# x in 64x64 quadrants of TensorE and a lag of four units, in a kernel of linear attention and a gated feed-forward layer

## The chip, the cores and the metric

One core of a Trainium2 chip. The metric is device time in microseconds (us), the median of several executions. Before: 284.53 us (four runs, 284.4 to 284.81).

Engines: PE is TensorE (PEld its weight loads), DVE is VectorE, ACT is ScalarE, POOL is GpSimd, SP issues transfers.

## The reference

```python
# q, k, v: (8 batches, 8 heads, 576 tokens, 64); w_in: 512 x 2048; w_out: 2048 x 512
q_s = softmax(q, over the 64 features);  k_s = softmax(k, over the 576 tokens)
kv  = einsum('bhsd,bhse->bhde', k_s, v)            # one 64x64 matrix a head
x   = einsum('bhsd,bhde->bhse', q_s, kv)           # -> 4608 tokens x 512
h   = x @ w_in
out = (h * sigmoid(beta * h)) @ w_out
```

The work is cut into nine chunks of 512 tokens: 512 tokens of each of the eight batches, and one chunk of the eight 64-token tails. Names used below: `kv` is the kv product of a batch; `x` the product of q and kv of a chunk, which gives the input of the feed-forward layer transposed, in four tiles kt of 128 features; `h j` (j = 0 to 15) are four matmuls that make 128 of the 2048 hidden features; `b j` are four matmuls that add hidden features j to four output accumulators (`acc`). Between h and b, ACT makes `th` (tanh of h) and DVE makes `g` from th and h.

## The kernel before

The kernel uses eight banks of PSUM. Four hold acc; of the others two serve h (tag "h") and two serve kv and x (tag "att").

x was made from weights of two heads side by side on the diagonal of a 128x128 tile whose other two quarters are zero (`kvp`), one full-array matmul for each kt:

```python
def xpe(c, j, tag):
    t = x_ps[c, j] = ps.tile([P, MAIN], F32, tag=bank(tag), ...)
    if c < B:
        nc.tensor.matmul(t[:], kvp[:, c, j, :], qsT[c][:, :, j, :])     # 128x128, 512 columns
        return
    for b in range(B):                                                  # the tails, 64 columns each
        i, e = divmod(b, 2)
        nc.tensor.matmul(t[:, ds(b * TAIL, TAIL)], kvp[:, b, j, :], qsT[B][:, i, j, ds(e * TAIL, TAIL)])
```

kv ran in two column tiles (128 rows by 64 columns), 40 matmuls of 65 columns:

```python
for i in range(R + 1):
    for e in range(2):
        hd = 2 * j + e
        nc.tensor.matmul(t[e * D : (e + 1) * D, jl, 0:D1], ek[...], va[...],
                         start=(i == 0), stop=(i == R), tile_position=(0, e * D))
```

A chunk made its 16 h units with b two units behind, and in between, through `side`, the softmaxes, kv and x of the next chunk:

```python
# h0 b14' h1 b15' h2 h3 b0 b1 h4 b2 h5 b3 ... h15 b13      (' = of the chunk before)
if u == 9 + (n == 1) and kb < B:
    kv_mm(kb, 0, n=HP); kv_norm(kb, 0, n=HP)
if 11 <= u < 15:                                  # one x after each of b9, b10, b11, b12
    j = u - 11
    x_mm(qc, j, nc.scalar if j % 2 == 0 else nc.vector)
```

The softmax here doesn't subtract the row's maximum and nothing guards it: scores larger than these inputs give would overflow.

Of the kernel before, what the change touches and what calls it, by code (L numbers as in the profile page):

```python
# [17 lines left out]
def kernel(  # L18
# [10 lines left out]
    nc = tc.nc  # L29
# [15 lines left out]
    FIX, LASTMAIN, COLT, XT4 = True, True, True, False  # L45
# [20 lines left out]
    kvp = const.tile([P, B, HP, P], BF16, name="kvp")  # L66
# [22 lines left out]
    def load_q(b, parts=1, only=None):  # L89
        if b not in q_st:  # L90
            q_st[b] = stage.tile([P, H, R * D], F32, tag="q_st", bufs=2, name=f"q_st{b}")
        t = q_st[b]
        src = q[b, :, 0:MAIN, :].rearrange("h (p i) d -> p h (i d)", i=R)
        n = H // parts
        for s in range(parts) if only is None else (only,):
            nc.sync.dma_start(t[:, s * n : (s + 1) * n, :], src[:, s * n : (s + 1) * n, :])  # L96
# [125 lines left out]
    def q_exp(b, s, n=2):  # L222
        if s == 0:
            eq[b] = work.tile([P, R, H, D], BF16, tag="eq", bufs=2, name=f"eq{b}")
        m = H // n
        nc.scalar.activation(  # L226
# [30 lines left out]
    HB, AB = ["b3", "b0"], ["b1", "b2"]  # L257
# [53 lines left out]
    def kv_mm(b, jj, n=2, tag="att"):  # L311
        t = ps.tile([P, n, D1 if b < NW or COLT else 2 * D1], F32, tag=bank(tag), bufs=1, name=f"kv{b}_{jj}")
        att_of[b, jj] = t
        for jl in range(n):
            j = n * jj + jl
            if b < NW:
                for i in range(RW):
                    for e in range(2):
                        r = slice(e * D, (e + 1) * D)
                        nc.tensor.matmul(  # L320
                            t[r, jl, 0:D1],
                            ek[b][r, j, ds(i * D, D)],
                            va[b][r, j, i, :],
                            start=(i == 0),
                            stop=(i == RW - 1),
                            tile_position=(e * D, e * D),
                        )
                continue
            if COLT:
                for i in range(R + 1):  # L330
                    for e in range(2):
                        hd = 2 * j + e
                        nc.tensor.matmul(  # L333
                            t[e * D : (e + 1) * D, jl, 0:D1],
                            ek[b][:, i, hd, :] if i < R else ekt[(b // 2) % 2][:, ds(hd * D, D)],
                            va[b][:, i, hd, :] if i < R else vt[(b // 2) % 2][:, b % 2, hd, :],
                            start=(i == 0),
                            stop=(i == R),
                            tile_position=(0, e * D),
                        )  # L340
                continue
            for i in range(R):
                nc.tensor.matmul(
                    t[:, jl, :],
                    ek[b][:, i, 2 * j : 2 * j + 2, :].rearrange("p h d -> p (h d)"),
                    va[b][:, i, 2 * j : 2 * j + 2, :].rearrange("p h d -> p (h d)"),
                    start=(i == 0),
                    stop=False,
                )
            nc.tensor.matmul(  # L350
                t[:, jl, :],
                ekt[(b // 2) % 2][:, ds(j * P, P)],
                vt[(b // 2) % 2][:, b % 2, 2 * j : 2 * j + 2, :].rearrange("p h d -> p (h d)"),
                start=False,
                stop=True,
            )

    def kv_norm(b, jj, n=2):
        t = att_of.pop((b, jj))
        rk = work.tile([P, n, 1], F32, tag="rk", bufs=2, name=f"rk{b}_{jj}")  # L360
        nc.vector.reciprocal(rk[:], t[:, :, D : D + 1])
        for e in range(2):
            r = slice(e * D, (e + 1) * D)
            dst = kvp[r, b, n * jj : n * jj + n, e * D : (e + 1) * D]
            src = t[r, :, 0:D] if b < NW or COLT else t[r, :, e * D1 : e * D1 + D]
            nc.vector.tensor_tensor(dst, src, rk[r].to_broadcast((D, n, D)), ALU.mult)
# [3 lines left out]
    def xpe(c, j, tag):  # L370
        t = x_ps[c, j] = ps.tile([P, MAIN], F32, tag=bank(tag), bufs=1, name=f"x{c}_{j}")
        if c < B:
            nc.tensor.matmul(t[:], kvp[:, c, j, :], qsT[c][:, :, j, :])  # L373
            return
        for b in range(B):
            i, e = divmod(b, 2)
            nc.tensor.matmul(  # L377
                t[:, ds(b * TAIL, TAIL)],
                kvp[:, b, j, :],
                qsT[B][:, i, j, ds(e * TAIL, TAIL)],  # L380
            )
# [6 lines left out]
    def x_mm(c, j, eng, tag="att"):  # L388
        xpe(c, j, tag)
        xev(c, j, eng)  # L390

    xp_of = {}

    def x_tiles(c):
        xp_of[c] = [ps.tile([P, HP, MAIN // 2], BF16, tag=bank("att"), bufs=1, name=f"xp{c}_{e}") for e in range(2)]
        for j in range(HP):
            for th in range(2):
                for e in range(2):
                    r = slice(e * D, (e + 1) * D)
                    nc.tensor.matmul(  # L400
                        xp_of[c][e][th * D : (th + 1) * D, j, :],
# [544 lines left out]
```

## Time and profile before

| | |
|---|---|
| time | 284.53 us |
| span of the profile | 282.9 us |
| PE busy | 97% |
| period of a middle chunk | 29.35 us |
| its 128 matmuls of h and b | 27.61 us |
| its kv block | 0.86 us |
| its four x | 0.86 us |

From the page of the kernel before: the busy times (engine, us, share of the span, instructions) and the chain of work that ended last.

```profile
PE 275.2 (97%) x1653; PEld 130.1 (46%) x1681; DVE 176.5 (62%) x274; ACT 164.9 (58%) x243; POOL 39.6 (14%) x60
...
PE 93%; DMA 3%; SPq 1%; POOL 1%; issue 1%; ACT 0%
PE h L425 44%; PE acc L473 42%; DMA v_st<-in_v_dram 3%; PE x L373 2%; PE kv L333 2%; PE acc L465 1%; PE kv L292 1%; SPq L122 1%; POOL va L161 0%; POOL w_in_b L161 0%; PE tp L273 0%; PE x L377 0%; SPq L119 0%; SPq L593 0%; SPq L96 0%
```

The chain is PE almost from end to end. "PE busy" alone would not say that PE is at its limit, since the matmuls' ends are modelled. The start times do. This is the PE timeline of the kernel before, around the kv block and the x of one middle chunk: start, us, engine, line, operation, count.

```profile
90.92 1.03 PE L473 MATMUL acc<-w_out_b,g 128*128 128x512 bf16 x4
91.88 0.32 PE L333 MATMUL kv<-va,ek 128*64 128x65 bf16 x8
...
92.50 0.20 PE L333 MATMUL kv<-vt,ekt 128*64 128x65 bf16 x2
92.64 1.04 PE L425 MATMUL h<-xT,w_in_b 128*128 128x512 bf16 x3
...
96.10 0.38 PE L373 MATMUL x<-qsT,kvp 128*128 128x512 bf16 x1
96.32 1.03 PE L425 MATMUL h<-xT,w_in_b 128*128 128x512 bf16 x4
97.18 1.03 PE L473 MATMUL acc<-w_out_b,g 128*128 128x512 bf16 x4
98.05 0.38 PE L373 MATMUL x<-qsT,kvp 128*128 128x512 bf16 x1
```

Read the differences of the first column. Four matmuls start in 97.18 - 96.32 = 0.86 us, 0.2157 us each: no gap. Below, a full matmul's "stream" is these 0.2157 us from its start. (The Trainium skill, TensorE: Matmul & The Clock Gate, section "Wait — 56ns, not 53.3ns?", gives N / 2.4 GHz plus about 2.5 ns for warm back-to-back matmuls, 215.7 ns at 512 columns. This trace agrees to the nanosecond.) An x takes 96.32 - 96.10 = 0.22, like any other full matmul, though half its weights are zeros. The kv block is entered 91.88 - (90.92 + 0.863) = 0.10 us later than a matmul of the same mode would have been, and left 0.13 us after its last start. That is what changing the tiling mode costs. A "x3" where four must be is a record missing from the trace, not a matmul left out.

The table by stretches (us, then each engine's busy time and instructions, PE clock, DMA share, GB/s) shows the slack of the others in a middle chunk:

```profile
core 0: us, PE busy (x) PEld busy (x) DVE busy (x) ACT busy (x) POOL busy (x), PEclk, DMA share, GB/s
...
93.68:123.03 29.35, 29.19 (x170) 13.55 (x172) 19.14 (x30) 17.43 (x25) 2.65 (x3) 1.00 0.63 171
```

### The profile page before, as it was taken

The numbers are of one execution on the slowest core, as the hardware profiler recorded it, in microseconds if no ns is written. First come the engines' busy times: TensorE is split into PE (matmuls) and PEld (weight loads), VectorE is DVE, ScalarE is ACT, GpSimd is POOL, SyncE is SP. The second block draws the span as 40 slices with busy tenths as digits, with TensorE's granted clock in tenths as the row PEclk, the third lists the DMA queues.
The fourth block names the chain that finished last, engine by engine and source line by source line (L and its number), as shares of the span: only waits on it lengthen the run. The fifth ranks groups of instructions, "written<-read, shape, count | busy, mean of one in ns | idle before, by whom it ended". The sixth has DMA issues, their size and how long they took to land.

```text
span 282.9 us, 4278 instructions
## 1 busy us (share of the span) xinstructions
PE 275.2 (97%) x1653; PEld 130.1 (46%) x1681; DVE 176.5 (62%) x274; ACT 164.9 (58%) x243; POOL 39.6 (14%) x60
## 2 busy tenths in 40 slices
PE   8799999999999999999999999999999999999995
PEld 3444454444444544444444444444445444445543
DVE  2864586975487547845785468655964595454361
ACT  2874987954496348644873568346935563554451
POOL 1565235220030003000300030000300000000000
PEclk9999999999999999999999999999999999999999
DMA  7999999929930993099407941599354033005003
GB/s 231 392 393 395 380 392 312 292 44 290 225 151 12 271 272 155 0 227 315 163 5 177 307 158 65 114 233 234 128 88 137 1 148 62 14 0 148 0 2 148
DMA packets 54868, 50.09 MB, mean 177 GB/s; under 512 B 26296, under 2 KB 47040, under 8 KB 54848
## 3 DMA queue, kind: packets, MB, share of 16 engines
q1 hardware_dynamic: 54704, 49.69, 58.7%
q8 instruction: 13, 0.21, 0.3%
q10 hardware_dynamic: 144, 0.13, 0.1%
q14 instruction: 7, 0.06, 0.1%
HBM read 36.71 MB, written 9.44 MB: 163 GB/s over the span
## 4 chain that ended last, share of the span: by engine, by line
PE 93%; DMA 3%; SPq 1%; POOL 1%; issue 1%; ACT 0%
PE h L425 44%; PE acc L473 42%; DMA v_st<-in_v_dram 3%; PE x L373 2%; PE kv L333 2%; PE acc L465 1%; PE kv L292 1%; SPq L122 1%; POOL va L161 0%; POOL w_in_b L161 0%; PE tp L273 0%; PE x L377 0%; SPq L119 0%; SPq L593 0%; SPq L96 0%
## 5 line engine op out<-in xcount | busy, mean ns | idle before, releaser
L435 ACT ACTIVATE th<-h,beta_t 128x512 bf16<-128x512 f32 x144 | 98.2, 688 | 93.4 <-PE h L425 87.2
L439 DVE SCALAR_TENSOR_TENSOR g<-th,h 128x512 bf16<-128x512 bf16 x144 | 97.7, 683 | 84.6 <-ACT th L435 82.7
L425 PE MATMUL h<-xT,w_in_b 128*128 128x512 bf16 x560 | 142.4, 379 | 1.0
L473 PE MATMUL acc<-w_out_b,g 128*128 128x512 bf16 x548 | 138.8, 379 | 0.5 <-issue 0.2
L425 PEld LDWEIGHTS <-w_in_b 128*128 128x128 bf16 x576 | 55.6, 98 | 64.4 <-POOL w_in_b L161 0.4
L473 PEld LDWEIGHTS <-g 128*128 128x128 bf16 x560 | 54.5, 98 | 65.6 <-DVE g L439 0.5
L161 POOL CAST va<-v_st 128x2048 bf16<-128x2048 f32 (+2 forms) x14 | 16.9, 1207 | 149.7 <-DMA v_st<-in_v_dram 149.4
L237 DVE TENSOR_REDUCE rq<-eq 128x16 f32<-128x1024 bf16 x18 | 21.9, 1216 | 7.6 <-ACT eq L226 7.6
L243 DVE TENSOR_TENSOR eq<-eq,rq 128x1024 bf16<-128x1024 bf16 x18 | 22.3, 1239 | 0.1
L226 ACT ACTIVATE eq<-q_st 128x1024 bf16<-128x1024 f32 x16 | 16.1, 1049 | 4.5 <-DMA q_st<-in_q_dram 4.5
L159 ACT CAST xT<-x 128x512 bf16<-128x512 f32 x18 | 10.6, 588 | 6.6 <-PE x L373 5.8
L161 DVE COPY o<-acc 128x512 f32<-128x512 f32 (+1 forms) x19 | 12.1, 670 | 3.4 <-PE acc L473 3.2
L159 ACT COPY o<-acc 128x512 f32<-128x512 f32 (+1 forms) x18 | 9.6, 576 | 7.0 <-PE acc L473 2.9
L161 DVE CAST xT<-x 128x512 bf16<-128x512 f32 x18 | 12.3, 685 | 0.9 <-PE x L373 0.9
L180 ACT ACTIVATE ek<-k_st 128x1024 bf16<-128x1024 f32 x12 | 12.6, 1047 | 0.0
L373 PE MATMUL x<-qsT,kvp 128*128 128x512 bf16 x32 | 11.6, 379 | 0.1
L546 PE MATMUL warm<-kvp 128*128 128x512 bf16 x31 | 8.5, 442 | 1.2 <-DVE kvp L626 1.2
L161 POOL CAST w_in_b<-w_in 128x512 bf16<-128x512 f32 (+1 forms) x12 | 7.5, 650 | 3.0 <-DMA w_in<-in_moe_w_in_dram 2.9
L161 POOL CAST w_out_b<-w_out 128x1024 bf16<-128x1024 f32 x4 | 5.0, 1248 | 7.5 <-DMA w_out<-in_moe_w_out_dram 7.5
L546 PEld LDWEIGHTS <-kvp 128*128 128x128 bf16 x31 | 3.3, 111 | 5.8 <-issue 2.2
L173 ACT ACTIVATE ek<-k_st 128x576 bf16<-128x576 f32 x8 | 5.2, 686 | 1.0 <-DMA k_st<-in_k_dram 1.0
L333 PEld LDWEIGHTS <-ek 128*64 128x64 bf16 x192 | 4.1, 111 | 2.5 <-ACT th L435 2.5
(45 smaller groups left out, 84.6 us busy)
## 6 DMA issues: line engine op xcount, KB each, us to landing
q_st<-in_q_dram SPq DMA_DIRECT2D x7, 1024.0 KB, 6.6
out_dram<-o SPq DMA_DIRECT2D x14, 512.0 KB, 3.4
k_st<-in_k_dram SPq DMA_DIRECT2D x6, 1024.0 KB, 9.5
v_st<-in_v_dram SPq DMA_DIRECT2D x6, 1024.0 KB, 10.6
w_in<-in_moe_w_in_dram SPq DMA_DIRECT2D x6, 512.0 KB, 9.4
v_st<-in_v_dram SPq DMA_DIRECT2D x8, 288.0 KB, 8.5
w_out<-in_moe_w_out_dram SPq DMA_DIRECT2D x4, 512.0 KB, 9.3
w_out<-in_moe_w_out_dram SPq DMA_DIRECT2D x2, 1024.0 KB, 11.2
```

The lines of the kernel that those rows point to most:

```text
L159: eng.copy(dst, src)
L161: eng.tensor_copy(dst, src)
L180: nc.scalar.activation(ek[b][:, :, h, :].rearrange("p i h d -> p h i d"), k_st[b][:, h, 0 : R * D].rearrange("p h (i d) -> p h i d", i=R), ...
L226: nc.scalar.activation(eq[b][:, :, s * m : (s + 1) * m, :].rearrange("p i h d -> p h i d"), q_st[b][:, s * m : (s + 1) * m, :].rearrange(" ...
L237: nc.vector.tensor_reduce(rq[b][:, 0, :, h], eq[b][:, :, h, :], axis=AX.X, op=ALU.add)
L243: eng.tensor_tensor(eq[b][:, :, h, :], eq[b][:, :, h, :], rq[b][:, 1, :, h].unsqueeze(3).to_broadcast((P, R, m, D)), ALU.mult,)
L373: nc.tensor.matmul(t[:], kvp[:, c, j, :], qsT[c][:, :, j, :])
L425: nc.tensor.matmul(h[:], w_unit(j, kt), x_of(c)[:, kt, :], start=(kt == 0), stop=(kt == KT - 1),)
L435: nc.scalar.activation(th[:], h_of[c, j][:], ACTF.Tanh, scale=beta_t[:, j : j + 1])
L439: nc.vector.scalar_tensor_tensor(out=g[:], in0=th_of.pop((c, j))[:], scalar=1.0, in1=h_of[c, j][:], op0=ALU.add, op1=ALU.mult)
L473: nc.tensor.matmul(acc[st][:], g[:, ds(st * P, P)], w_out_b[:, j, :], start=(j == 0), stop=(j == NJ - 1),)
L546: nc.tensor.matmul(t[:], kvp[:, B - 1, 0, :], kvp[:, B - 1, :, :].rearrange("p j r -> p (j r)"))
```

## The change

Intent: make x in a quarter of the array per head, so that no zero is multiplied and four heads run at once. The Trainium skill (TensorEngine Tiling (Array Packing), section "Gotcha 1: PSUM Pressure") says that different row tiles cannot write the same PSUM bank at once. Each half of x therefore writes two banks, and all of x four, so it takes both h banks and both att banks. To leave room around that, x is done once, after b12, and b lags h by four units. The order of heads in q and in kv is changed to fit the quadrants, and the loads, casts and the hand-written order of chunk 0 and of batch 1 are new. Cut to its core:

```diff
-    kvp = const.tile([P, B, HP, P], BF16, name="kvp")
+    kvp = const.tile([P, NW, HP, P], BF16, name="kvp")          # batches 0 and 1 only
+    kvq = const.tile([P, B - NW, HP, D], BF16, name="kvq")      # no zeros
-    HB, AB = ["b3", "b0"], ["b1", "b2"]
+    HB, AB = ["b0", "b1"], ["b2", "b3"]
+    def x_quad(c):
+        xr = [ps.tile([P, MAIN], F32, tag=bank(("att", "h")[kt // 2]), ...) for kt in range(KT)]
+        for b in range(B) if c == B else (c,):
+            ...                                                  # batches 0, 1 of the tails: full array, kvp
+            for m in range(2):
+                for a in range(2):
+                    for r in range(2):
+                        rr = slice(r * D, (r + 1) * D)
+                        qx = qsT[c][rr, :, 2 * m + a, :]
+                        nc.tensor.matmul(
+                            xr[2 * m + r][a * D : (a + 1) * D, cols],
+                            kvq[rr, b - NW, 2 * m + a, :],
+                            qx[:, i, ds(e * TAIL, TAIL)] if c == B else qx,
+                            tile_position=(r * D, a * D),
+                        )
+        for kt in range(KT):
+            evac((nc.scalar, nc.vector)[kt % 2], x_of(c)[:, kt, :], xr[kt][:])
 # kv_mm: head of column tile r, pair j
-                        hd = 2 * j + e
+                    hd = j // 2 * 4 + 2 * r + j % 2
 # kv_norm: one multiplication on 128 partitions instead of two on 64
 # batch 1 (one example of the new hand order)
-    kvz_mm(1, 3, "b1", 1)
-    vz_cast(1, 2, G, part=0)
-    mm_b(0, 14)
     ...
-    kvz_mm(1, 2, "b0", 1)
+    mm_b(0, 14)
+    ...
+    kvz_mm(1, 3, "b0", 1)
+    kvz_mm(1, 2, "b1", 1)
 # the order of a chunk; "a" takes an att bank, p is b15 of the chunk before
+        2: 'h0 p15 h1 h2a h3a b0 h4 b1 h5 b2 h6a h7 b3 h8 b4 h9 b5 h10 b6 h11 b7 h12 b8 h13 b9 h14 b10 h15 b11 b12 x0 b13 b14',
```

More of the change, by code (lines that the diff above doesn't have):

```diff
@@ L44 @@
     LAG = 2
-    FIX, LASTMAIN, COLT, XT4 = True, True, True, False
+    FIX, LASTMAIN = True, True
     NCH = B + 1
@@ L94, in load_q @@
         n = H // parts
+        if b >= NW:
+            for m in range(2):
+                for r in range(2):
+                    nc.sync.dma_start(
+                        t[:, 4 * m : 4 * m + 4, :].rearrange("p (s r) x -> p s r x", r=2)[:, :, r, :],
+                        src[:, 4 * m + 2 * r : 4 * m + 2 * r + 2, :],
+                    )
+            return
         for s in range(parts) if only is None else (only,):
@@ L225, in q_exp @@
         m = H // n
+        if b == B:
+            hs = slice(s * m, (s + 1) * m)
+            e_, q_ = eq[b][:, :, hs, :], q_st[b][:, hs, :].rearrange("p h (i d) -> p i h d", i=R)
+            lo = NW // 2
+            nc.scalar.activation(e_[:, 0:lo], q_[:, 0:lo], ACTF.Exp)
+            for r in range(2):
+                nc.scalar.activation(
+                    e_[:, lo:R].rearrange("p i (s r) d -> p i s r d", r=2)[:, :, :, r, :],
+                    q_[:, lo:R, 2 * r : 2 * r + 2, :],
+                    ACTF.Exp,
+                )
+            return
         nc.scalar.activation(
@@ L309, in kvz_norm @@
             )
-    def kv_mm(b, jj, n=2, tag="att"):
-        t = ps.tile([P, n, D1 if b < NW or COLT else 2 * D1], F32, tag=bank(tag), bufs=1, name=f"kv{b}_{jj}")
-        att_of[b, jj] = t
-        for jl in range(n):
-            j = n * jj + jl
-            if b < NW:
-                for i in range(RW):
-                    for e in range(2):
-                        r = slice(e * D, (e + 1) * D)
-                        nc.tensor.matmul(
-                            t[r, jl, 0:D1],
-                            ek[b][r, j, ds(i * D, D)],
-                            va[b][r, j, i, :],
-                            start=(i == 0),
-                            stop=(i == RW - 1),
-                            tile_position=(e * D, e * D),
-                        )
-                continue
-            if COLT:
-                for i in range(R + 1):
-                    for e in range(2):
-                        hd = 2 * j + e
-                        nc.tensor.matmul(
-                            t[e * D : (e + 1) * D, jl, 0:D1],
-                            ek[b][:, i, hd, :] if i < R else ekt[(b // 2) % 2][:, ds(hd * D, D)],
-                            va[b][:, i, hd, :] if i < R else vt[(b // 2) % 2][:, b % 2, hd, :],
-                            start=(i == 0),
-                            stop=(i == R),
-                            tile_position=(0, e * D),
-                        )
-                continue
-            for i in range(R):
-                nc.tensor.matmul(
-                    t[:, jl, :],
-                    ek[b][:, i, 2 * j : 2 * j + 2, :].rearrange("p h d -> p (h d)"),
-                    va[b][:, i, 2 * j : 2 * j + 2, :].rearrange("p h d -> p (h d)"),
-                    start=(i == 0),
-                    stop=False,
-                )
-            nc.tensor.matmul(
-                t[:, jl, :],
-                ekt[(b // 2) % 2][:, ds(j * P, P)],
-                vt[(b // 2) % 2][:, b % 2, 2 * j : 2 * j + 2, :].rearrange("p h d -> p (h d)"),
-                start=False,
-                stop=True,
-            )
@@ L358, in kv_norm, with kv_mm @@
-    def kv_norm(b, jj, n=2):
-        t = att_of.pop((b, jj))
-        rk = work.tile([P, n, 1], F32, tag="rk", bufs=2, name=f"rk{b}_{jj}")
-        nc.vector.reciprocal(rk[:], t[:, :, D : D + 1])
-        for e in range(2):
-            r = slice(e * D, (e + 1) * D)
-            dst = kvp[r, b, n * jj : n * jj + n, e * D : (e + 1) * D]
-            src = t[r, :, 0:D] if b < NW or COLT else t[r, :, e * D1 : e * D1 + D]
-            nc.vector.tensor_tensor(dst, src, rk[r].to_broadcast((D, n, D)), ALU.mult)
+    def kv_mm(b):
+        t = att_of[b] = ps.tile([P, HP, D1], F32, tag=bank("att"), bufs=1, name=f"kv{b}")
+        for j in range(HP):
+            for i in range(R + 1):
+                for r in range(2):
+                    hd = j // 2 * 4 + 2 * r + j % 2
+                    nc.tensor.matmul(
+                        t[r * D : (r + 1) * D, j, :],
+                        ek[b][:, i, hd, :] if i < R else ekt[(b // 2) % 2][:, ds(hd * D, D)],
+                        va[b][:, i, hd, :] if i < R else vt[(b // 2) % 2][:, b % 2, hd, :],
+                        start=(i == 0),
+                        stop=(i == R),
+                        tile_position=(0, r * D),
+                    )
@@ new lines, in kv_norm @@
+    def kv_norm(b):
+        t = att_of.pop(b)
+        rk = work.tile([P, HP, 1], F32, tag="rk", bufs=2, name=f"rk{b}")
+        nc.vector.reciprocal(rk[:], t[:, :, D:D1])
+        nc.vector.tensor_tensor(kvq[:, b - NW], t[:, :, 0:D], rk[:].to_broadcast((P, HP, D)), ALU.mult)
+    def x_quad(c):
+        xr = [ps.tile([P, MAIN], F32, tag=bank(("att", "h")[kt // 2]), bufs=1, name=f"x{c}_{kt}") for kt in range(KT)]
+        for b in range(B) if c == B else (c,):
+            i, e = divmod(b, 2)
+            cols = ds(b * TAIL, TAIL) if c == B else slice(0, MAIN)
+            if b < NW:
+                for j in range(HP):
+                    nc.tensor.matmul(
+                        xr[j][:, cols], kvp[:, b, j, :], qsT[c][:, i, j, ds(e * TAIL, TAIL)]
+                    )
+                continue
+            for m in range(2):
+                for a in range(2):
+                    for r in range(2):
+                        rr = slice(r * D, (r + 1) * D)
+                        qx = qsT[c][rr, :, 2 * m + a, :]
+                        nc.tensor.matmul(
+                            xr[2 * m + r][a * D : (a + 1) * D, cols],
+                            kvq[rr, b - NW, 2 * m + a, :],
+                            qx[:, i, ds(e * TAIL, TAIL)] if c == B else qx,
+                            tile_position=(r * D, a * D),
+                        )
+        for kt in range(KT):
+            evac((nc.scalar, nc.vector)[kt % 2], x_of(c)[:, kt, :], xr[kt][:])
@@ L371, in xpe @@
         t = x_ps[c, j] = ps.tile([P, MAIN], F32, tag=bank(tag), bufs=1, name=f"x{c}_{j}")
-        if c < B:
-            nc.tensor.matmul(t[:], kvp[:, c, j, :], qsT[c][:, :, j, :])
-            return
-        for b in range(B):
-            i, e = divmod(b, 2)
-            nc.tensor.matmul(
-                t[:, ds(b * TAIL, TAIL)],
-                kvp[:, b, j, :],
-                qsT[B][:, i, j, ds(e * TAIL, TAIL)],
-            )
+        nc.tensor.matmul(t[:], kvp[:, c, j, :], qsT[c][:, :, j, :])
     def xev(c, j, eng, part=None):
@@ L386, in xev @@
         evac(eng, x_of(c)[:, j, cols], x_ps[c, j][:, cols])
-    def x_mm(c, j, eng, tag="att"):
-        xpe(c, j, tag)
-        xev(c, j, eng)
-    xp_of = {}
-    def x_tiles(c):
-        xp_of[c] = [ps.tile([P, HP, MAIN // 2], BF16, tag=bank("att"), bufs=1, name=f"xp{c}_{e}") for e in range(2)]
-        for j in range(HP):
-            for th in range(2):
-                for e in range(2):
-                    r = slice(e * D, (e + 1) * D)
-                    nc.tensor.matmul(
-                        xp_of[c][e][th * D : (th + 1) * D, j, :],
-                        kvp[r, c, j, e * D : (e + 1) * D],
-                        qsT[c][r, 2 * th : 2 * th + 2, j, :],
-                        tile_position=(e * D, th * D),
-                    )
-    def x_evac(c, jh):
-        for e in range(2):
-            for th in range(2):
-                evac(
-                    nc.scalar if th == 0 else nc.vector,
-                    x_of(c)[e * D : (e + 1) * D, 2 * jh : 2 * jh + 2, th * 256 : th * 256 + 256],
-                    xp_of[c][e][th * D : (th + 1) * D, 2 * jh : 2 * jh + 2, :],
-                )
     h_of = {}
@@ L545, in warm @@
         for _ in range(n):
-            nc.tensor.matmul(t[:], kvp[:, B - 1, 0, :], kvp[:, B - 1, :, :].rearrange("p j r -> p (j r)"))
+            nc.tensor.matmul(t[:], xT[2][:, 0, 0:P], xT[2][:, 0, :])
     V, A, G = nc.vector, nc.scalar, nc.gpsimd
@@ L596 @@
     w_load("in", 0, 0)
-    w_load("in", 0, 3)
     w_load("in", 0, 1)
     w_load("in", 0, 2)
+    w_load("in", 0, 3)
     w_load("in", 1, 0)
@@ L606 @@
     w_load("out", 1)
-    load_kv(v_st, v, 1, "v_st", [0])
+    w_load("in", 3, 1)
     w_load("in", 3, 0)
-    w_load("in", 3, 1)
     load_q(1, 2, 0)
@@ L614 @@
     load_kv(k_st, k, 1, "k_st", [0])
+    load_kv(v_st, v, 1, "v_st", [0])
     load_kv(k_st, k, 1, "k_st", [1])
     w_load("out", 3, 0)
+    w_load("out", 3, 1)
+    load_kv(k_st, k, 1, "k_st", [2])
+    load_kv(v_st, v, 1, "v_st", [3])
     load_kv(k_st, k, 1, "k_st", [3])
-    w_load("out", 3, 1)
-    load_kv(v_st, v, 1, "v_st", [3])
-    load_kv(k_st, k, 1, "k_st", [2])
     load_kv(v_st, v, 1, "v_st", [2])
@@ L624 @@
     load_kv(v_st, v, 2, "v_st")
-    nc.vector.memset(kvp[:, B - 1], 0.0)
+    nc.vector.memset(xT[2][:, 0, :], 0.0)
     make_identity(nc, identity[:])
     make_identity(nc, ident8[:])
-    nc.vector.memset(kvp[:, 0 : B - 1], 0.0)
+    nc.vector.memset(kvp[:], 0.0)
     v_buf(0)
@@ L641 @@
     vz_cast(0, 0, G)
-    warm(13, tag="acc2")
+    warm(18, tag="acc2")
     tpe(0, 0, "acc3")
@@ L666 @@
     tpe(0, 2, "b3")
-    w_castk(0, 3, G)
+    w_castk(0, 1, G)
     q_ev(0, 3, A)
@@ L671 @@
     xpe(0, 1, "acc3")
-    hpe(0, 2, [0], "b1")
+    hpe(0, 1, [0], "b1")
     q_ev(0, 2, A)
-    w_castk(0, 1, G)
-    hpe(0, 1, [0], "b2")
+    hpe(0, 2, [0], "b2")
     xev(0, 1, V)
     hpe(0, 0, [0], "acc0")
+    w_castk(0, 2, A)
     xpe(0, 3, "acc2")
-    w_castk(0, 2, G)
+    w_castk(0, 3, G)
     xpe(0, 2, "acc1")
     xev(0, 3, V)
+    hpe(0, 0, [1])
+    xev(0, 2, A)
     hpe(0, 1, [1])
-    xev(0, 2, A)
-    hpe(0, 0, [1])
     hpe(0, 3, [1])
@@ L704 @@
     g_dve(0, 1)
-    hpe(0, 6, [0], "b1")
+    hpe(0, 6, [0], "b2")
     hpe(0, 5, [2])
@@ L708 @@
     hpe(0, 5, [3])
-    hpe(0, 7, [0], "b2")
+    hpe(0, 7, [0], "b1")
     th_act(0, 0)
@@ L712 @@
     g_dve(0, 3)
+    hpe(0, 6, [2])
+    hpe(0, 6, [3])
+    th_act(0, 5)
     w_cast("out", 0, 0, G)
     hpe(0, 7, [1])
+    g_dve(0, 0)
     hpe(0, 7, [2])
-    th_act(0, 5)
-    hpe(0, 6, [2])
-    g_dve(0, 0)
-    hpe(0, 6, [3])
-    hpe(0, 7, [3])
+    hpe(0, 4, [0], "b0")
+    th_act(0, 6)
     g_dve(0, 5)
-    th_act(0, 6)
-    hpe(0, 4, [0], "b0")
-    w_cast("out", 0, 1, G)
+    hpe(0, 4, [1])
+    hpe(0, 4, [2])
     mm_b(0, 0)
-    th_act(0, 7)
+    w_cast("out", 0, 1, A)
     g_dve(0, 6)
     mm_b(0, 1)
-    g_dve(0, 7)
     w_castk(2, 0, G)
@@ L733 @@
     mm_b(0, 3)
-    w_castk(2, 2, G)
-    w_castk(2, 3, G)
-    hpe(0, 4, [1])
-    hpe(0, 4, [2])
+    w_castk(2, 2, A)
+    w_castk(2, 3, A)
     hpe(0, 4, [3])
-    hpe(0, 8, [0, 1, 2, 3], "b1")
+    hpe(0, 7, [3])
     th_act(0, 4)
     hpe(0, 9, [0, 1, 2, 3], "b2")
+    th_act(0, 7)
     g_dve(0, 4)
-    th_act(0, 8)
+    hpe(0, 8, [0, 1, 2, 3], "b3")
+    th_act(0, 9)
+    g_dve(0, 7)
     w_cast("out", 1, 0, A)
     hpe(0, 11, [0, 1, 2, 3], "b0")
-    g_dve(0, 8)
-    vz_cast(1, 0, G, part=0)
-    hpe(0, 10, [0, 1, 2, 3], "b1")
-    th_act(0, 9)
-    th_act(0, 11)
-    w_cast("in", 3, 0, G)
-    g_dve(0, 9)
+    g_dve(0, 9)
+    hpe(0, 10, [0, 1, 2, 3], "b1")
+    th_act(0, 8)
+    w_cast("in", 3, 1, G)
+    th_act(0, 11)
+    g_dve(0, 8)
     mm_b(0, 4)
@@ L755 @@
     g_dve(0, 11)
+    w_cast("in", 3, 0, G)
     mm_b(0, 5)
-    vz_cast(1, 0, A, part=1)
     th_act(0, 10)
     mm_b(0, 6)
-    w_cast("in", 3, 1, A)
     g_dve(0, 10)
-    mm_b(0, 7)
     q_exp(1, 0)
@@ L767 @@
     th_act(0, 13)
-    hpe(0, 14, [0, 1, 2, 3], "b2")
-    w_cast("out", 2, 0, A)
-    w_cast("out", 2, 1, G)
-    g_dve(0, 13)
-    hpe(0, 15, [0, 1, 2, 3], "b3")
-    th_act(0, 12)
+    mm_b(0, 7)
+    th_act(0, 12)
+    g_dve(0, 13)
+    w_cast("out", 2, 1, G)
+    w_cast("out", 2, 0, A)
+    hpe(0, 14, [0, 1, 2, 3], "b2")
     q_mul(1, 0)
+    hpe(0, 15, [0, 1, 2, 3], "b0")
     q_exp(1, 1)
+    g_dve(0, 12)
     mm_b(0, 8)
-    g_dve(0, 12)
     vz_cast(1, 1, G)
     th_act(0, 14)
-    mm_b(0, 9)
@@ L781 @@
     q_sum(1, 1)
     th_act(0, 15)
+    mm_b(0, 9)
+    kz_exp(1, 0)
+    vz_cast(1, 0, G, part=0)
     mm_b(0, 10)
-    kz_exp(1, 0)
     g_dve(0, 15)
+    vz_cast(1, 0, A, part=1)
+    kz_exp(1, 1)
+    g_dve(0, 14)
     mm_b(0, 11)
-    kz_exp(1, 1)
     q_mul(1, 1)
-    w_cast("out", 3, 0, G)
     tpe(1, 0, "b0")
+    w_cast("out", 3, 0, A)
     tpe(1, 1, "b1")
+    kvz_mm(1, 0, "b2", 2)
+    q_ev(1, 1, V)
+    kvz_mm(1, 1)
     q_ev(1, 0, A)
-    kvz_mm(1, 0, "b3", 2)
-    g_dve(0, 14)
-    kvz_mm(1, 1)
@@ L796 @@
-    q_ev(1, 1, A)
-    tpe(1, 3, "b0")
-    kz_exp(1, 3)
-    kvz_norm(1, 0, 2)
-    mm_b(0, 12)
-    w_cast("out", 3, 1, A)
-    tpe(1, 2, "b1")
-    xpe(1, 1, "b2")
-    vz_cast(1, 3, G, part=0)
-    q_ev(1, 2, V)
-    xpe(1, 0, "b3")
-    vz_cast(1, 3, A, part=1)
-    mm_b(0, 13)
-    xev(1, 1, V)
-    q_ev(1, 3, A)
-    kz_exp(1, 2)
-    kvz_mm(1, 3, "b1", 1)
-    vz_cast(1, 2, G, part=0)
+    tpe(1, 3, "b1")
+    kvz_norm(1, 0, 2)
+    tpe(1, 2, "b3")
+    w_cast("out", 3, 1, G)
+    mm_b(0, 12)
@@ L814 @@
+    q_ev(1, 2, A)
+    q_ev(1, 3, V)
+    kz_exp(1, 2)
+    xpe(1, 1, "b0")
+    xpe(1, 0, "b1")
+    xev(1, 1, V)
+    mm_b(0, 13)
+    vz_cast(1, 3, A, part=1)
+    vz_cast(1, 3, G, part=0)
+    xev(1, 0, A)
+    kz_exp(1, 3)
     mm_b(0, 14)
     vz_cast(1, 2, A, part=1)
+    vz_cast(1, 2, G, part=0)
+    kvz_mm(1, 3, "b0", 1)
+    kvz_mm(1, 2, "b1", 1)
     kvz_norm(1, 3)
-    xev(1, 0, A)
-    kvz_mm(1, 2, "b0", 1)
     mm_b(0, 15)
     kvz_norm(1, 2)
-    xpe(1, 3, "b1")
+    xpe(1, 3, "b0")
@@ L822 @@
     store(0, 0)
-    xpe(1, 2, "b0")
+    hpe(1, 0, [0], "b2")
     xev(1, 3, V)
-    hpe(1, 0, [0], "b2")
     hpe(1, 0, [1])
+    xpe(1, 2, "b1")
+    hpe(1, 1, [0], "b3")
+    store(0, 1)
     xev(1, 2, A)
-    hpe(1, 2, [0], "b3")
-    store(0, 1)
+    hpe(1, 1, [1])
+    hpe(1, 2, [0], "b0")
     hpe(1, 2, [1])
-    hpe(1, 1, [0], "b1")
     hpe(1, 0, [2])
+    store(0, 2)
     hpe(1, 0, [3])
-    store(0, 2)
-    hpe(1, 1, [1])
     hpe(1, 1, [2])
+    store(0, 3)
     th_act(1, 0)
-    store(0, 3)
@@ L839 @@
     hpe(1, 1, [3])
     hpe(1, 2, [2])
+    hpe(1, 2, [3])
     th_act(1, 1)
-    hpe(1, 2, [3])
+    hpe(1, 3, [0], "b1")
     g_dve(1, 0)
-    hpe(1, 3, [0], "b0")
     hpe(1, 3, [1])
+    hpe(1, 3, [2])
     th_act(1, 2)
-    hpe(1, 3, [2])
+    hpe(1, 3, [3])
     g_dve(1, 1)
-    hpe(1, 3, [3])
     mm_b(1, 0)
@@ L887, in side @@
         if u == 9 + (n == 1) and kb < B:
-            kv_mm(kb, 0, n=HP)
-            kv_norm(kb, 0, n=HP)
-        if 11 <= u < 15:
-            j = u - 11
-            x_mm(qc, j, nc.scalar if j % 2 == 0 else nc.vector)
+            kv_mm(kb)
+            kv_norm(kb)
         if u == 9 and n + 2 < NCH:
@@ L899 @@
     HOLD = 8
+    SEQ = {
+        1: 'h4 b2 h5 h6a b3 h7 b4 h8a h9 b5 h10 b6 h11 b7 h12 b8 h13 b9 h14 b10 h15 b11 b12 x0 b13 b14',
+        2: 'h0 p15 h1 h2a h3a b0 h4 b1 h5 b2 h6a h7 b3 h8 b4 h9 b5 h10 b6 h11 b7 h12 b8 h13 b9 h14 b10 h15 b11 b12 x0 b13 b14',
+        B: 'h0 p15 h1 h2a b0 h3 b1 h4 b2 h5 b3 h6 b4 h7 b5 h8 b6 h9 b7 h10 h11 h12a h13 h14 h15a',
+    }
     for n in range(1, NCH):
         c = order[n]
-        for j in range(LEAD if n == 1 else 0, NJ):
-            if not (n > 1 and j == 3):
-                mm_a(c, j, tag="att" if n == B and j > HOLD + LAG and j % 3 == 0 else None)
-            if n > 1 and j == 2:
-                mm_a(c, 3)
-            if n == B and j >= HOLD + LAG:
-                continue
-            if j >= LAG:
-                mm_b(c, j - LAG)
-            else:
-                finish_b(order[n - 1], NJ + j - LAG)
-            side(n, j)
+        for w in SEQ.get(n, SEQ[2]).split():
+            kind, j = w[0], int(w[1:].rstrip("a"))
+            if kind == "h":
+                mm_a(c, j, tag="att" if w[-1] == "a" else None)
+                side(n, j)
+            elif kind == "b":
+                mm_b(c, j)
+            elif kind == "p":
+                finish_b(order[n - 1], j)
+            elif kind == "x":
+                x_quad(order[n + 1])
     for st in range(R + 1):
```

## The prediction

> **What bounds it now.** TensorE: 97% of the 282.9 us span on the page, 93% of the chain of waits. By the table of stretches each middle chunk takes 29.35 us. In the PE timeline four 512-column matmuls start 0.863 us apart, so a chunk's 128 h and acc matmuls take 27.61 us. The other 1.74 are four x matmuls (0.86) and the kv block (91.785 to 92.64, 0.86). The list of waits has no PE entry above 1.2 us, all in the first 14 us. Only fewer PE cycles help; VectorE and ScalarE are busy 65% and 60% of a chunk.
>
> **What mode changes cost.** Kv runs in column tiles: it starts 0.10 us after the matmul before would have let the next go, and h follows 0.13 us after it. Between, 40 starts come 15.8 ns apart, two tiles at a time. Batch 1's blocks in 64x64 tiles show the same. The Trainium skill (TensorEngine Tiling (Array Packing), Key Properties) says a change of tiling mode drains TensorE; this trace agrees, 0.23 us for in and out.
>
> **What the change does.**
> 1. x of batches 2 to 7: eight 64x64 matmuls of 512 columns in four quadrants, for four full ones that half multiply zeros. That page gives 64x64 as four independent tiles; the trace shows only pairs together. Estimate: entry 0.10, first round 0.22, second with spacing 0.24, exit 0.12: 0.68 us against 0.86. Saves 0.18, six times: 1.1 us.
> 2. Tail x: 32 matmuls of 64 columns cost 0.95 us (that chunk takes 28.56 and has no kv). After: 8 x 29 ns + 48 x 8 to 16 ns + 0.23 = 0.85 to 1.2 us. Loses about 0.1.
> 3. Batch 1: kv of pairs 3 and 2 becomes one block: one mode change less, -0.2 us.
> 4. The smaller kvp memset and the joined normalization relieve VectorE, off the path. New load and cast orders: PE is nearly dense from 15.2 us already; I give them 0.2 us. The start hangs on the last v of batch 0, landed at 12.5 us, which stays.
> 5. x once, after b12, takes both h and both att banks. By durations in the trace h15's bank is free 1.6 us after h15; b11 and b12 (1.73 us) stand between. The four evacuations, two on each engine (0.59, 0.69), end 1.55 us after x; b13 and b14 cover 1.73. No wait, or tenths.
> 6. Lag four: h units bunch early in a chunk. With stores, exp and q work in order, my hand schedule has g7 free h9's bank 0.1 us before h9, thin again. Chunk 1's kv moves to about 60 us; v of batch 2 is cast by 58.5: it just fits.
>
> **Sum.** -1.1 + 0.1 - 0.2 - 0.2, and +0.3 for thin margins: -1.1 us, so 283.3 us. Range 281.9 to 284.7. Faster by over 2%: 0.02; within: 0.96; slower: 0.02.
>
> **What would show it.** Period near 29.17 us; x starts in two bunches of four 0.22 us apart; 0.6 to 0.75 us between b12's end and b13's start. PE gaps before x, h0 and h9 below 0.1 us. Th and g totals unchanged; the end (3.3 us after the last matmul) unchanged.
>
> **What would make it wrong.** Only two quadrants at once: x costs 1.1 us and the kernel is 1.4 slower. Weight loads not hidden between the rounds: 0.1 each. Bank handover at x or h9 waits: up to 0.3 us a chunk, 2 in all. Or drains hide behind long matmuls and x costs 0.5 us: 282.2.

## The result, and the profile after

283.07 us (four runs, 282.97 to 283.58) against 284.53. The ratio is 0.9951, with a 95% interval of 0.9934 to 0.9968: 0.5% less, within the 2% that count as the same.

From the page after, the same lines:

```profile
PE 273.8 (97%) x1705; PEld 128.1 (46%) x1734; DVE 172.4 (61%) x269; ACT 162.9 (58%) x249; POOL 35.9 (13%) x57
...
PE 91%; DMA 6%; issue 1%; SPq 1%; POOL 0%; ACT 0%
```

The bound is the same, PE. The PE timeline after, around the x of a middle chunk:

```profile
99.98 1.89 PE L445 MATMUL acc<-w_out_b,g 128*128 128x512 bf16 x7
101.80 0.63 PE L369 MATMUL x<-qsT,kvq 64*64 64x512 bf16 x8
102.36 1.90 PE L445 MATMUL acc<-w_out_b,g 128*128 128x512 bf16 x8
104.09 1.03 PE L397 MATMUL h<-xT,w_in_b 128*128 128x512 bf16 x4
```

b11 and b12 are eight matmuls from 99.98 on (one record is missing), so their stream ends at 99.98 + 8 x 0.2157 = 101.70. From there to b13 at 102.356 are 0.65 us; that is all of x, against 0.86 before. h0 of the next chunk follows b13 and b14 with no gap. The single starts behind the 101.80 line, read from the trace's records:

```
x       101.799 101.802 101.805 101.808      102.039 102.042 102.044 102.048
b13     102.356
```

Four matmuls start within 9 ns, and the next four 0.24 us later: four quadrants, two rounds. The evacuations of this x, from the ACT and the DVE timeline:

```profile
102.25 1.07 ACT L168 CAST xT<-x 128x512 bf16<-128x512 f32 x2 [1.39 <-PE x L369]
102.29 1.29 DVE L170 CAST xT<-x 128x512 bf16<-128x512 f32 x2 [0.70 <-PE x L369]
```

The first of each engine begins about 0.45 us after x's first start, on the signals of the first round (semaphore updates at 102.23 and 102.26). The last ends at 103.58, 1.31 us after the second round's streams (102.048 + 0.216 = 102.26). The stretch of one period, from kv block to kv block:

```profile
core 0: us, PE busy (x) PEld busy (x) DVE busy (x) ACT busy (x) POOL busy (x), PEclk, DMA share, GB/s
88.85:118.00 29.15, 28.89 (x174) 13.20 (x177) 18.56 (x29) 16.87 (x25) 2.65 (x3) 1.00 0.63 172
```

29.15 against 29.35: 0.20 us a chunk, nearly the whole 0.21 of x.

The tails, after:

```profile
216.59 1.89 PE L445 MATMUL acc<-w_out_b,g 128*128 128x512 bf16 x7
218.32 0.40 PE L360 MATMUL x<-qsT,kvp 128*128 128x64 bf16 x8
218.64 0.57 PE L369 MATMUL x<-qsT,kvq 64*64 64x64 bf16 x48
219.38 1.68 PE L445 MATMUL acc<-w_out_b,g 128*128 128x512 bf16 x7 [0.16 <-issue]
```

Eight matmuls of b13 and b14 should follow, and seven are recorded. With the missing first one put at 219.38 - 0.22 = 219.16, the tails take 219.16 - 218.32 = 0.84 us. Before, 32 starts 29 ns apart took 0.93.

Adding up, with the first acc matmul of chunk 1 (50.344 before, 50.105 after) and PE's last start (279.298, 277.763) as marks:

| part | gain in the profile |
|---|---|
| start, up to the first acc of chunk 1 | 0.24 |
| from there to PE's last start | 1.30 |
| ... of which six quadrant blocks, 6 x 0.20 | 1.2 |
| ... of which tails | 0.09 |
| after PE's last start (3.64 and 3.48) | 0.16 |
| span | 1.69 |

The times differ by less than these spans do (1.46 us), because single runs of one kernel differ by some tenths.

### The profile page after: what moved, and what is told of

It reads as the page before. It is cut to its first block, busy times and chain, and to the rows that moved or that the text cites. A ratio compares the mean times of both kernels' runs of the same rounds, so it can differ in the third digit from the quotient of the medians. Undisturbed runs are those within 1.5% of the kernel's fastest.

```text
span 281.2 us, 4409 instructions
## 1 busy us (share of the span) xinstructions
PE 273.8 (97%) x1705; PEld 128.1 (46%) x1734; DVE 172.4 (61%) x269; ACT 162.9 (58%) x249; POOL 35.9 (13%) x57
## 4 chain that ended last, share of the span: by engine, by line
PE 91%; DMA 6%; issue 1%; SPq 1%; POOL 0%; ACT 0%
PE acc L445 43%; PE h L397 43%; DMA v_st<-in_v_dram 3%; DMA w_in<-in_moe_w_in_dram 3%; PE kv L338 2%; PE x L369 1%; PE acc L437 1%; PE kv L313 0%; PE tp L294 0%; PE x L382 0%; POOL w_in_b L170 0%; SPq L128 0%; SPq L131 0%; SPq L105 0%; SPq L150 0%
## 5 line engine op out<-in xcount | busy, mean ns | idle before, releaser
L411 DVE SCALAR_TENSOR_TENSOR g<-th,h 128x512 bf16<-128x512 bf16 x144 | 96.7, 679 | 83.6 <-ACT th L407 81.7
L445 PE MATMUL acc<-w_out_b,g 128*128 128x512 bf16 x538 | 136.1, 379 | 2.0 <-issue 1.3
L445 PEld LDWEIGHTS <-g 128*128 128x128 bf16 x560 | 53.4, 98 | 65.7 <-issue 2.5
L170 POOL CAST va<-v_st 128x2048 bf16<-128x2048 f32 (+2 forms) x14 | 16.0, 1144 | 146.2 <-DMA v_st<-in_v_dram 145.9
L168 ACT CAST xT<-x 128x512 bf16<-128x512 f32 x18 | 9.9, 589 | 11.1 <-PE x L369 10.1
L518 PE MATMUL warm<-xT 128*128 128x512 bf16 x36 | 9.6, 433 | 1.2 <-DVE xT L598 1.2
L518 PEld LDWEIGHTS <-xT 128*128 128x128 bf16 x36 | 3.8, 109 | 6.4 <-issue 2.2
L168 ACT CAST w_out_b<-w_out 128x1024 bf16<-128x1024 f32 x5 | 5.3, 1052 | 0.3 <-DMA w_out<-in_moe_w_out_dram 0.3
L437 PE MATMUL acc<-w_out_b,g 128*128 128x256 bf16 x32 | 5.0, 273 | 0.0
```

The lines of the kernel that those rows point to most:

```text
L168: eng.copy(dst, src)
L170: eng.tensor_copy(dst, src)
L411: nc.vector.scalar_tensor_tensor(out=g[:], in0=th_of.pop((c, j))[:], scalar=1.0, in1=h_of[c, j][:], op0=ALU.add, op1=ALU.mult)
L445: nc.tensor.matmul(acc[st][:], g[:, ds(st * P, P)], w_out_b[:, j, :], start=(j == 0), stop=(j == NJ - 1),)
L518: nc.tensor.matmul(t[:], xT[2][:, 0, 0:P], xT[2][:, 0, :])
```

## The experiments

Eleven different kernels ran, two of them twice (e9 is e6 again, a0 the change again). "Period" is from kv block to kv block in the middle of the run, "start" the first acc matmul of chunk 1, "rest" from there to PE's last start.

| run | median us | ratio to before | period | start | rest |
|---|---|---|---|---|---|
| before | 284.53 | | 29.35 | 50.34 | 228.95 |
| after | 283.07 | 0.9951 | 29.15 | 50.11 | 227.66 |
| e1, full-array x | 284.66 | 0.9999 | 29.35 | 50.51 | 228.95 |
| e2, other issue order | 283.18 | 0.9942 | 29.16 | 50.07 | 227.72 |
| e3, x in two blocks | 284.74 | 0.9995 | 29.38 | 50.63 | 229.04 |
| e7, two quadrants | 286.04 | 1.003 | 29.58 | 49.91 | 230.21 |
| e4, x earlier | 286.97 | 1.0065 | 29.64 | 50.68 | 231.29 |
| e5, x later | 284.16 | 0.9963 | 29.30 | 49.81 | 228.86 |
| e8, lag of two | 292.48 | 1.0269 | 30.37 | 49.99 | 236.85 |
| e6, old start | 283.42 | 0.9949 | 29.15 | 50.45 | 227.66 |
| e9, old start again | 283.63 | 0.9954 | 29.15 | 50.71 | 227.66 |
| e10, one kv split | 283.95 | 0.9972 | 29.15 | 50.97 | 227.66 |
| a0, after again | 283.32 | 0.9951 | 29.15 | 49.86 | 227.66 |

### e1: the new orders with the old x

```diff
-    kvp[P, NW, ...], kvq[P, B - NW, HP, D]; eight quadrant matmuls; new head order
+    kvp[P, B, HP, P]; for j in range(HP): nc.tensor.matmul(xr[j][:, cols], kvp[:, b, j, :], ...)   # same place, same banks
```

> The changed kernel's orders, lag, banks and place of x kept; only x goes back to four full-array matmuls from zero-padded weights (and 32 small ones for the tails), heads in the old order. Theory (the gain of the steady chunks is the array time of x alone): x window from the end of b12's stream to the first matmul of b13 0.86 us instead of 0.65, period 29.36 instead of 29.15, tails 0.93 instead of 0.85; in all 0.21 x 6 + 0.08 = 1.3 us slower than the change, 284.4 us. Rival (the lag of four and the head orders bring the gain): the period stays at 29.15 and the time within 0.2 us of 283.1.

Measured: 284.66 us; the period is 29.35, and "rest" is 228.95, that of the kernel before to the hundredth. PE timeline of this run:

```profile
102.31 1.03 PE L363 MATMUL x<-qsT,kvp 128*128 128x512 bf16 x4
103.17 1.89 PE L436 MATMUL acc<-w_out_b,g 128*128 128x512 bf16 x8
```

x takes 0.86 us again. The lag of four, the new chunk orders and the banks bring nothing by themselves: the 1.3 us of "rest" are the array time of x. As to the order of heads, the rival is not tested here, because e1 puts that back too; e3 and e7 below keep the new order and lose the gain all the same. So the rival fell. The end after PE's last start is 3.63 us here, as before the change (3.64), and 3.48 to 3.49 in every other run: the 0.16 us gained there go with what e1 puts back (x, the order of heads, the normalization of kv), for a reason that stays open.

### e2: the eight matmuls in another order

```diff
-    for m, a, r in product:  (0,0,0) (0,0,1) (0,1,0) (0,1,1) (1,0,0) ...
+    for a, r in ((0, 0), (1, 1), (1, 0), (0, 1)): for m in range(2):
```

> The same eight quadrant matmuls of x (batches 2 to 7), issued in another order: both matmuls of a quadrant one behind the other (quadrants 00, 11, 10, 01), so that in-order issue leaves at most two quadrants running. The result stays right. Theory (what counts is how many quadrants run together): starts in five steps of 0.22 us instead of two, x window about 1.28 us instead of 0.65, the kernel 0.63 x 6 = 3.8 us slower than the change, 286.8 us, slower than before too. Rival (half the work is saved by leaving out the zeros, whatever the order): as the change, 283.1 us.

Measured: 283.18 us, period 29.16. My theory's numbers failed. The starts, from the trace's records:

```
x       101.773 101.780 101.787 101.793      102.013 102.020 102.027 102.033
```

Two bunches of four again, only 7 ns apart within a bunch instead of 3. The premise that failed is "in-order issue leaves at most two quadrants running". So this run does not speak against four quadrants at once: it shows that issue order did not limit it, and that the run could not tell the two theories apart. What did the separating is e7.

### e7: two quadrants instead of four (wrong result on purpose)

```diff
-    xr[2 * m + r][a * D : (a + 1) * D, cols], ..., tile_position=(r * D, a * D)
+    xr[2 * m + r][r * D : (r + 1) * D, cols], ..., tile_position=(r * D, r * D)     # tails as before
```

> Wrong result on purpose: the eight x matmuls of batches 2 to 7 all go to two quadrants (00 and 11), four to each; half of x is not written and its evacuation copies only the written 64 partitions. Same count and shapes of instructions. Theory (four quadrants run at once, and the block costs 0.22 us plus 0.215 us a round): four rounds, x window 0.22 + 4 x 0.215 = 1.08 us against 0.65, period 29.58, 0.43 x 6 = 2.6 us slower than the change, 285.7 us. Rival (the array takes the 64x64 matmuls two at a time anyway, or the saving comes from the halved work): window stays 0.65, time 283.1.

Measured: 286.04 us, period 29.58 as expected. PE timeline and starts:

```profile
100.21 1.89 PE L447 MATMUL acc<-w_out_b,g 128*128 128x512 bf16 x7
102.03 1.05 PE L370 MATMUL x<-qsT,kvq 64*64 64x512 bf16 x8
103.01 1.68 PE L447 MATMUL acc<-w_out_b,g 128*128 128x512 bf16 x7
```

```
x       102.029 102.032   102.269 102.272   102.485 102.488   102.700 102.704
```

Four rounds of two, 0.22 to 0.24 us apart; the same eight instructions now take 103.012 - 101.935 = 1.08 us, more than four full-array matmuls did. The saving is the number of quadrants that run together, not the halved work. With e2 this also says something of the order: as a quadrant takes one matmul at a time (e7), e2's first bunch must have held one of each quadrant, although its second instruction was for the quadrant of its first. The semaphore waits and updates that the trace keeps with each record agree in all six blocks (in the last, one of the waits for the att banks is absent, as it is in the change): e2's first bunch holds the two matmuls that wait for the att banks (issued first and third) and two of the four that signal (issued fifth to eighth), and the second bunch begins with the two that wait for the h banks (issued second and fourth). The signals did not pass one another: in the block shown all four come after the second bunch, from 102.43 on, where in the change two come at 102.23 and 102.26, after the first.

### e3: x in two blocks

```diff
-  ... b11 b12 x0 b13 b14          # x_quad: m = 0 and 1
+  ... b11 b12 x0 b13 x1 b14       # x0: m = 0, two att banks; x1: m = 1, two h banks
```

> x of batches 2 to 7 in two blocks of four quadrant matmuls, one after b12 and one after b13, two banks each; everything else as changed. Theory (a block pays about 0.19 to 0.23 us for going into the 64x64 mode and back, whatever its size): each block 0.09 + 0.24 + 0.09 = 0.42 us, 0.84 together against 0.65, so 0.19 x 6 = 1.1 us slower than the change, 284.2 us, and nothing left of the gain in the steady chunks. Rival (mode changes hide behind 512-column matmuls): both blocks together 0.65 to 0.7, time within 0.3 of 283.1.

Measured: 284.74 us, period 29.38. PE timeline:

```profile
100.73 1.89 PE L449 MATMUL acc<-w_out_b,g 128*128 128x512 bf16 x7
102.55 0.41 PE L373 MATMUL x<-qsT,kvq 64*64 64x512 bf16 x4
102.89 1.04 PE L449 MATMUL acc<-w_out_b,g 128*128 128x512 bf16 x4
103.86 0.41 PE L373 MATMUL x<-qsT,kvq 64*64 64x512 bf16 x4
104.20 1.04 PE L449 MATMUL acc<-w_out_b,g 128*128 128x512 bf16 x4
```

Each block takes from the end of the stream before (103.86's is 102.89 + 0.863 = 103.75) to the next b 0.44 us. One round costs 0.44, two 0.65 (after), four 1.08 (e7): these lie on a line of 0.22 us for going in and out and 0.215 a round. Two blocks of one round cost 0.88, what the four full matmuls cost. So the whole gain hangs on doing x in one block, and it is this that takes four banks at once. The time is 0.5 us above the expectation; in this profile 0.5 us lie in the start (50.63), which varies from run to run (below).

### e4 and e5: x one unit earlier, one unit later

```diff
-  h15 b11 b12 x0 b13 b14
+  h15 b11 x0 b12 b13 b14          # e4
+  h15 b11 b12 b13 x0 b14          # e5
```

> x one b unit earlier: h15 b11 x b12 b13 b14. Theory (x waits for the bank of h15, free 1.6 us after h15's stream ends; b11 covers 0.86): the second round of x, which takes the h banks, waits about 0.4 us, x window about 1.05 us, seven times, 2.9 us slower than the change, 286.0 us; VectorE's g of h15 named as what PE waits for. Rival (the margin is not what ties the place of x): within 0.3 us of 283.1.

> x one b unit later: h15 b11 b12 b13 x b14. Theory (the next h0 needs its bank, which the third evacuation frees, about 1.4 us after x's stream ends; b14 covers 0.86 and the way out of the mode 0.1): PE waits about 0.4 us before h0, seven times, 2.9 us slower than the change, 286.0 us. Rival: the evacuations are off the path whatever the place, within 0.3 us of 283.1.

Measured for e4: 286.97 us, period 29.64, so 0.49 us lost a chunk. The DVE timeline of e4, the g of h15:

```profile
101.97 0.69 DVE L411 SCALAR_TENSOR_TENSOR g<-th,h 128x512 bf16<-128x512 bf16 x1 [1.04 <-ACT th L407]
```

and its PE timeline around x:

```profile
102.00 1.11 PE L369 MATMUL x<-qsT,kvq 64*64 64x512 bf16 x8
103.05 2.76 PE L445 MATMUL acc<-w_out_b,g 128*128 128x512 bf16 x12
```

By the records, five x matmuls start by 102.245 and the last three at 102.711, right after g of h15 ends at 102.66. The bank of h15 holds up the second round, as expected, a tenth longer than I had put it.

Measured for e5: 284.16 us, period 29.30, so 0.15 us lost a chunk, where I expected 0.4. The PE timeline of e5:

```profile
102.50 0.63 PE L369 MATMUL x<-qsT,kvq 64*64 64x512 bf16 x8
103.06 1.04 PE L445 MATMUL acc<-w_out_b,g 128*128 128x512 bf16 x4
104.08 1.02 PE L397 MATMUL h<-xT,w_in_b 128*128 128x512 bf16 x4
```

and its ACT timeline, the two evacuations that ACT does:

```profile
102.96 1.07 ACT L168 CAST xT<-x 128x512 bf16<-128x512 f32 x2 [2.25 <-PE x L369]
```

b14's four matmuls end at 103.94, h0 starts at 104.08, after the two evacuations of ACT end at 104.03. The direction was right and the size not: the first evacuation starts 0.46 us after x's first start, where I had it at 0.66, 0.2 us after the end of x's last stream. Tiles kt 0 and 1 are complete after the first round (in e2, where kt 0 waits for the signal of the fifth matmul issued, the first evacuation starts 0.68 us after x's first start).

From these two, in estimate: in the change itself the bank of h15 is ready about 0.86 - 0.49 = 0.37 us before it would hold x up, and the evacuations about 0.86 - 0.15 = 0.71 us before they would hold h0 up.

### e8: the new x with the old lag

```diff
-  h0 p15 h1 h2a h3a b0 h4 b1 ... h15 b11 b12 x0 b13 b14
+  h0 p14 h1 p15 h2 h3 b0 b1 h4 b2 ... h15 b13 x0
```

> The changed x with the old lag of two: h15 b13 x, and then h0 b14 h1 b15 of the next chunk. Theory (the lag of four is there to put b units on both sides of x): x's second round waits 0.4 us for h15's bank, and h0 about 1.3 us for the evacuation of its bank, seven times 1.7 us: 12 us slower than the change, about 295 us, far slower than before. Rival (the lag matters little, because TensorE finds other work): under 286.

Measured: 292.48 us, period 30.37, 1.22 us more a chunk than the change, where I expected 1.7. PE timeline:

```profile
102.80 1.03 PE L445 MATMUL acc<-w_out_b,g 128*128 128x512 bf16 x3
103.75 1.11 PE L369 MATMUL x<-qsT,kvq 64*64 64x512 bf16 x8
105.54 1.02 PE L397 MATMUL h<-xT,w_in_b 128*128 128x512 bf16 x4 [0.67 <-ACT xT L168]
```

Both waits are there: x spreads over 1.11 instead of 0.63 us, and h0 waits for ACT's evacuation. The over-estimate is e5's, the early start of the evacuations. So the lag brings no time itself (e1) and is a condition: without it the quadrants cost 2.7% over before. Seven times 1.22 make 8.5 of the 9.2 us that "rest" grew; the other 0.7 I did not trace.

### e6, e9, e10 and a0: the start

e6 and e9 put the start of the kernel before in front of the changed chunks (banks renamed). e10 takes one kv block of batch 1 apart. a0 is the change unaltered.

```diff
 # e10
+    kvz_mm(1, 3, "b0", 1)
     mm_b(0, 14)
     ...
-    kvz_mm(1, 3, "b0", 1)
     kvz_mm(1, 2, "b1", 1)
```

> The changed kernel with the start of the kernel before (loads, casts and the hand order of chunk 0 and batch 1, up to the first acc matmuls of chunk 1); banks renamed so that they fit. Theory (the new start is worth 0.24 us, all else comes from x): first acc matmul of chunk 1 at 50.3 us instead of 50.1, time 283.3 us, the steady period 29.15 unchanged. Rival (the new start brings most of the 1.4 us): 284.0 or more.

> The changed kernel unaltered, as the standard for the two others of this call. 283.1 us; its first h between 14.8 and 15.7 us after the span's start, as in the runs so far, so that single times scatter by some 0.3 us.

> The changed kernel with the start of the kernel before, once more with more rounds, because one profile of each cannot tell 0.24 us: the start of several runs with the same start lay up to 0.5 us apart. Theory (one mode change fewer in batch 1 is worth about 0.23 us): 0.1 to 0.4 us slower than the unaltered changed kernel of this call. Rival (the new start brings nothing that holds): within 0.1 us of it.

> The changed kernel with the kv block of batch 1's last two pairs taken apart again, an acc unit between them (pair 3 one unit earlier, pair 2 as before); one mode change in and out more, nothing else. Theory (each costs 0.22 us wherever it stands): 0.2 us slower than the unaltered one in this call; in the profile, 0.22 us more between the first of the two blocks and the first acc matmul of chunk 1. Rival (in the start PE has slack that hides it): no difference in that stretch.

Measured: 283.42 (e6); 283.32, 283.63 and 283.95 (a0, e9, e10). The old start costs 0.3 us by the medians, but the ratios to before of a0 and e9 (0.9951 and 0.9954) do not separate them. The profiles do, once the start is cut in two. The first h comes anywhere from 14.76 to 15.79 us in kernels with the same start, so the absolute marks scatter. From the first kv of batch 1 to the first acc of chunk 1, though, it is 9.73 us in all nine profiles with the new start unaltered in that part, and 10.10, 10.09, 10.09 in the three with the old one. The new order of batch 1 is worth 0.37 us. From the first h to that kv it is 25.16 in seven profiles with the new start, against 24.96 to 25.02 with the old one in before and e6: 0.14 to 0.20 us are lost there. In the other profiles PE waits for weights on top (0.32 to 0.65 us, by the starts), as in the change's own:

```profile
16.11 3.40 PE L397 MATMUL h<-xT,w_in_b 128*128 128x512 bf16 x15
19.75 2.55 PE L397 MATMUL h<-xT,w_in_b 128*128 128x512 bf16 x11 [0.24 <-POOL w_in_b L170]
```

There PE stood from 19.35 to 19.75 us for a cast whose weights landed at 19.03. The landing varies with the run: with the new start it came at 18.9 to 19.0 us in the three profiles with this wait and at 17.6 to 17.9 in the seven without, among them e5, a0 and e7, which began h at 14.91 to 15.02, as early as e2 (15.04), which waited. With the old start it came at 18.9 to 19.3; e9 waited 0.65 us there and e6, which began h later (15.40 against 15.03), not at all. What moves the landing was not looked for.

e10's stretch from kv to acc is 10.49, 0.76 more than 9.73, not the 0.22 expected. Its PE timeline shows why:

```profile
42.93 1.03 PE L445 MATMUL acc<-w_out_b,g 128*128 128x512 bf16 x4
44.42 0.48 PE L313 MATMUL kv<-va,ek 64*64 64x65 bf16 x18 [0.47 <-ACT ek L182]
44.83 1.04 PE L445 MATMUL acc<-w_out_b,g 128*128 128x512 bf16 x4
45.80 0.47 PE L313 MATMUL kv<-va,ek 64*64 64x65 bf16 x18
46.21 1.04 PE L445 MATMUL acc<-w_out_b,g 128*128 128x512 bf16 x3
```

The earlier block ran into a wait for ACT's exp of k (0.47 idle), which I had not looked for. The way in and out of the second block reads 45.80 - (44.83 + 0.86) = 0.11 and 46.21 - (45.80 + 0.28) = 0.13, 0.24 together, as everywhere; but as a test of the sum the run is spoilt.

No run points to a version that beats the change: after the start its PE timeline shows, besides the mode changes at kv and x, a single wait, 0.15 us at 272.1.

## Why the prediction was right or wrong

The time was right: 283.3 predicted, 283.07 measured. Its parts were mis-sized in both directions:

1. "entry 0.10, first round 0.22, second with spacing 0.24, exit 0.12: 0.68 us against 0.86. Saves 0.18, six times: 1.1 us": right in mechanism, 0.65 us and 0.20 to 0.21 saved a block, 1.2 us in all. Four quadrants do run at once (e7 against after), though before the change the trace showed only pairs. e3 and e7 give the 0.22 us per block and 0.215 per round.
2. "Tail x ... Loses about 0.1": wrong in sign. It gained 0.09. The mis-sized term is 48 x 8 to 16 ns: the quadrant matmuls took the lower end, 48 starts in 0.38 us, four every 32 ns.
3. "Batch 1 ... -0.2 us": the mode change saved is there. "New load and cast orders ... I give them 0.2": the new order of batch 1 gained 0.37 us in all, but chunk 0 gave back 0.14 to 0.20, so the whole start is worth about 0.2 us, not 0.4.
4. "+0.3 for thin margins": nothing waited. The two margins at x were 0.37 us (h15's bank) and 0.71 us (the evacuations), not 0.1 to 0.2 (e4, e5). The step that failed is "The four evacuations ... end 1.55 us after x": the first two start when the first round is done, 0.2 us sooner than I had them, and h0 needs only its own bank at its start; the tile that DVE evacuates last is needed three matmuls later. In the change's trace the last evacuation ends 1.31 us after x, and ACT's second, which frees h0's bank, at 103.33, with h0 at 104.09. The bank of h15 did come free 1.6 us after h15's stream, as forecast (99.98 to 101.60); what was missed is that only the second round, from 102.04, takes it. At h9 the margin was 0.33 us instead of 0.1: g7, which frees its bank, ended at 116.72 and h9 began at 117.04.
5. "a change of tiling mode drains TensorE; this trace agrees, 0.23 us": the price held, 0.22, for 64x64 blocks of long matmuls too (e3); that it is a drain is the page's word, and no run here shows it apart. "Or drains hide behind long matmuls" did not happen.
6. "the end ... unchanged": it was 0.16 us shorter in the profile. From its issue to its last packet the last store took 1.41 us before and 1.39 after; the other 0.14 lie behind that packet. They go with what e1 puts back; why stays open.

Of these errors only the start's 0.2 was on the hopeful side; the +0.3 that did not come, 0.2 at the tails, 0.1 at x and 0.16 at the end all lay on the other. The terms add up to -1.1, and the profile gained 1.69. That the time came so near has some luck in it: the runs differ by 1.46 us, less than the profiles, and -1.1 from 284.53 would have been 283.43, not 283.3. A right total is no proof of its terms.

## What to carry to other kernels

Packing small products into quadrants pays by how many run together, minus a fixed price per mode change (here 0.22 us): count the blocks, not only the matmuls, since one block of two rounds gained 0.2 us and two blocks of one round gained nothing. A block that takes all the free PSUM banks needs independent work on both sides; give it that by lagging the consumer (here b behind h), and read the evacuations from the round that completes each bank. Where a kernel is bound by one engine without waits, sum that engine's start-to-start times, and check terms one by one, because a total near the mark can hide errors of some tenths in its terms.

## What the Trainium skill lacked or had wrong

- TensorEngine Tiling (Array Packing), "Key Properties" says that a mode change drains TensorE but gives no cost. Here: 0.22 us for in and out of a block of 64x64 tiles between full-array matmuls (blocks of one, two and four rounds: 0.44, 0.65, 1.08 us), and 0.23 for the column-tiled kv block.
- TensorE: Matmul & The Clock Gate, section "Wait — 56ns, not 53.3ns?", says without a limit that start-to-start never drops below about 25 ns. That does not hold from one quadrant to another, where starts come 3 ns apart and 48 matmuls of 64 columns start in 0.38 us, 8 ns on average. The page's own Part 3 ("Measured speedup vs the span model") counts about 4 ns for each further tile, so the sentence lacks only "within one tile": four starts every 32 ns are one every 32 ns for each quadrant.
- TensorE: Matmul & The Clock Gate, "Step-by-step: what each phase is for", says that matmuls stay in program order. In e2 two matmuls of each quadrant were issued one behind the other, and the starts still came in two bunches of four, 0.24 us apart, though a quadrant takes one at a time (e7). The semaphore waits and updates in the records put the matmuls issued second and fourth into the second bunch, behind later ones (e2, under e7): the starts in different quadrants passed one another. All four signals came after the second bunch, as the order of issue would have it.
